# Batch 0 of a gated linear attention and mixer kernel: the transposed input of the MLP summed in PSUM, the low-rank part added in the second MLP bank, a matmul group split by parity, and a new order table

## The chip, the cores and the metric

The kernel runs on one core of a Trainium2 chip. Five engines work side by side, each through its own instruction list from front to end: TensorE (PE, with its weight loads PEld), VectorE (DVE), ScalarE (ACT), GpSimd (POOL) and SyncE (SP, which here only starts transfers). ACT also starts some transfers. The metric is the device time of one execution in microseconds, the median over runs.

## The reference, cut to what matters

```python
# per batch b (4) and head h (8), over t = 0..767, head width 48
state = alpha[t, :, None] * state + outer(k[t], v[t])
y[t]  = q[t] @ state
# x: (4, 768, 384), the eight heads' y side by side
h  = x.T @ U @ V            # over time, rank 32
u  = x + h.T
ch = relu(u @ w_ch1) @ w_ch2   # 384 -> 1536 -> 384
out = u + ch
```

## The kernel before, in words

Four batches go through the same stages. Batch 0 is done wholly, and batch 1 for its first four of six steps, in "pair units": one unit is 256 time steps of four heads, folded to 128 partitions. All else is done in plain chunks of 128 time steps and eight heads.

A unit (`stage_pair`, names in brackets are the kinds in the order table) takes four loads of 192 KB: alpha, k, q, v. ACT takes the logarithm of alpha [ln]; PE sums it over time in a PSUM bank [pcum]; ACT takes two exponentials and the decay factors [exp, ptot]; k and q are scaled [rk, rq] on POOL or DVE; PE transposes both [tr], ACT or DVE copies them out [kqev]; PE forms the scores in two banks, one for the even heads of the unit and one for the odd ones [psc]; DVE multiplies each bank by the mask into the two halves of `pm` [mask, twice]; PE multiplies `pm` by v and adds the part from the state [py, pyi]; the result is copied to `xb`, which holds x [pyev].

`stage_mix` then does the low-rank part of a batch: PE forms x^T U in a bank [xu], which is copied to `utx`; for each chunk of 128 rows PE multiplies by V into a bank [hb], and DVE adds x to it into `ub` [u]. PE transposes `ub`, six tiles to a bank [utr], ACT or DVE copies that to `uT` [uev]. Batches 2 and 3 transpose `ub` by transfers [tu]. `mlp1` takes w1 tiles times `uT`, three matmuls of 384 columns for each of 24 tiles of a batch, and ACT or DVE takes the relu of each into `h1`. `mlp2` sums twelve matmuls of 384 columns for a chunk, in three groups of four, and DVE adds `ub` and writes the output tile [out], which SP stores.

The w1 matrix comes in four loads of 576 KB, each for three of the twelve column tiles of w1. They land as f32 in the space of the other batch's `h1`; three casts each, on ACT or POOL, make bf16 of them. A tile of `mlp1` needs all three casts of its group. SP starts these loads amid those of q, k, v and alpha.

What stands where is set by hand-held data: `Plan.add` collects the operations with their dependences, and `run` emits them in the order of `TABLE`, three characters an operation, the last of which names the engine. `SLOTS` gives each buffer its place in its pool. An entry `++` emits filler matmuls (L270) into a bank that is free. No scheduler runs: each engine follows the table's order, and an operation whose input is late holds up all that stands behind it on its engine.

Lines of the profile: L270 filler, L389 to L396 [pcum], L428 [tr], L452 [psc], L486 [pd, the unit's state], L535 [py], L592 and L620 the same in plain chunks, L702 [xu], L716 [hb], L717 [u], L736 [utr], L765 [mlp1], L775 and L777 [relu], L791 [mlp2], L797 [out], L277, L279 and L281 copies on ACT, DVE and POOL, L320 the weight loads, L350 and L357 those of pair units and plain chunks.

Of the kernel before, what the change touches and what calls it, by code (L numbers as in the profile page):

```python
# [20 lines left out]
GFAAMSDMDALGDCPDDADmPDoPEQDESPD1AAQSDEABMSGJGDpAD3PGZAETDD5DDFPEUPDGDGIGDqAGbPDNPEVPGDGDOPD6P++BDsAGcADHDEWPEXAD4DD7PD8D
DPPDRAEYDGKPGMAD9PAYSGLPGNDACGADPD+PD-PEADGRPGSDDQAAEAEBAGOPGPDEZPEaPBTSGfGGwAGeAGdAEbAGyPG1ABNSGTD++BG0AEqPGQDBRSEoPGhP
GVPErDEkPGgGGWPGzABQAEcPEiPGjAEpDElDGiPGaGEsPHJAAUSAOGGXAEePEjDEtAAPGGkDGYAEdDHLPBOSHMAHNAEfDEmPGlPEnDANGGoPEgPGpDFGPGmD
GqDFHDFIPATABVSGnDFKPARGEhAFLAEwPExAASGFMPFNAE4PE2PAaGFQPE5DEyPBXSG2GBUSAZAFRDAbAFAPFJAE0PAcSE3ABSABZSFEPFFAGrDHOAG4PG6A
G3DHPDE1DFBAEuPHRPHTDFOPHQGEzDFPDG5PHiAFcPAXAFaPEvDG7AFdAAVAHSPHUDGsPGtPGuDBYSGvAG8PG+DAWGAhSBWSGxGGUGBaSAmSHVPBfSBrSG-P
FbAHkPHmAHoAFWPHADHBGE6PHXDH4AHnAFSPHlAG9DHqGFYPFTDH6PE7DH7AH8AHWDE+PHsPHuDHCDHpGE8PHKAFXAFZAHrPHtDFUPFVABbSE-AE9DHEPAgA
HFPHGPHYPHZDAfGBtSBjSHHDHvPHdPHIDHwDH+GIAPFCPAeGHaGAdAH9GHePFePHbDAiABcSHcDHxDICDFDAFkPF2PH-PIBDF8PIDPAlAHfPAjGAkGF9PBeS
HgAFwPBhSIFDHDGIEDHjABnSHyPH2PH3AH5AHzDH0DF3PFlPH1DIGPHhAApAFfPIHAIIPFxPIJAIQPISPAoGIKPAnGIRDITDAqGF+PFyPILDIMPINDFgPIYP
IZDF-DFzDF4PKCAKEPLBABkSIWPKFABzSJuAIXDIUPIOPIVAIPDKXAFmPFnDIaPBqSIbDJwPJxAF5DJ1DIiPKZPJvAIjAKdAI0PBlSFhDKGABdSAIGJyAJEP
JFABvSB1SIgPKKGJ2GI1AI+PI-AKIAIyPI4PKsAI5AIzAJGPIhDBiSI6PI7AJ0AJzAImPIqPKHAIrAInAKaAJKPIwPKDGJ+PJHAIkPKbAKuPKwAJIPLDPJLD  # L30
# [826 lines left out]
```

## Time and profile before

| what | value |
|---|---|
| runs | 159.13, 157.86, 158.62 us |
| median | 158.62 us |
| span of the profiled execution | 156.8 us |
| PE busy | 148.8 us (95%) |
| DVE, ACT, POOL busy | 107.6, 90.0, 61.4 us |
| moved by DMA | 31.53 MB |

The page gives the profiled execution by its span, from its first instruction to its last; a time of its own is not given. The median of the three runs lies 1.8 us above that span. A PE matmul is drawn with its pipeline, so that a row's mean duration is longer than what the next one has to wait; the spacing is read from the chain of waits, where a run of matmuls of one line stands as one piece.

### The profile page before, as it was taken

How to read it: one execution, taken by the hardware profiler on the slowest of the kernel's cores; microseconds unless marked ns; L12 is line 12 of the kernel's file. 1: busy time of each engine (PE TensorE's matmuls, PEld its weight loads, DVE VectorE, ACT ScalarE, POOL GpSimd, SP SyncE). 2: the span in 40 equal slices, each digit the busy share in tenths (PEclk: the TensorE clock that was granted, in tenths of full speed). 3: DMA queues.
4: the chain of work that ended last, by engine and by line, in shares of the span. 5: the costliest groups of instructions: out<-in, count | busy, mean ns of one | idle time of the engine just before them, and what ended most of it. 6: DMA issues, size and time to landing. Idle time of an engine off the chain costs nothing.

```text
span 156.8 us, 4413 instructions
## 1 busy us (share of the span) xinstructions
PE 148.8 (95%) x1715; PEld 97.7 (62%) x1715; DVE 107.6 (69%) x236; ACT 90.0 (57%) x234; POOL 61.4 (39%) x95
## 2 busy tenths in 40 slices
PE   2878999999999999999999999999999999999992
PEld 0456678666767656666668666665667555556662
DVE  6038899987899628816588976885989580673162
ACT  3678889986978272999958585379232202450000
POOL 8285995756088600136679261052623000000000
PEclk9999999999999999999999999999999999999999
DMA  5999999999988989989989996897976346345625
GB/s 145 319 323 326 268 301 313 344 265 268 280 239 193 270 161 191 189 169 211 208 169 214 134 222 119 169 181 145 176 144 151 105 87 139 127 129 151 199 100 201
DMA packets 98291, 31.53 MB, mean 201 GB/s; under 512 B 91968, under 2 KB 98240, under 8 KB 98272
## 3 DMA queue, kind: packets, MB, share of 16 engines
q1 hardware_dynamic: 92464, 29.11, 80.6%
q10 hardware_dynamic: 5808, 2.16, 5.2%
q8 instruction: 13, 0.21, 0.6%
q14 instruction: 6, 0.05, 0.1%
HBM read 23.79 MB, written 4.72 MB: 182 GB/s over the span
## 4 chain that ended last, share of the span: by engine, by line
PE 84%; DMA 8%; DVE 4%; ACT 1%; issue 1%; ACTq 0%; DVEq 0%
PE ps L791 30%; PE ps L765 29%; DMA io<-in_alpha_dram 8%; PE ps L716 3%; PE ps L620 3%; PE ps L592 2%; PE ps L687 2%; PE ps L428 2%; PE ps L535 2%; PE ps L558 2%; PE ps L682 1%; PE ps L736 1%; PE ps L452 1%; PE ps L643 1%; PE ps L702 1%; DVE rkq L411 1%
## 5 line engine op out<-in xcount | busy, mean ns | idle before, releaser
L791 PE MATMUL ps<-w_sb,h1t 128*128 128x384 bf16 (+2 forms) x300 | 53.1, 319 | 0.0
L765 PE MATMUL ps<-uT,w_sb 128*128 128x384 bf16 x288 | 51.0, 326 | 0.1
L775 ACT ACTIVATE h1t<-ps 128x384 bf16<-128x384 f32 x58 | 27.2, 509 | 19.1 <-PE ps L765 19.0
L791 PEld LDWEIGHTS <-h1t 128*128 128x128 bf16 x300 | 27.3, 97 | 15.9 <-issue 0.6
L765 PEld LDWEIGHTS <-w_sb 128*128 128x128 bf16 x288 | 27.0, 98 | 16.3 <-issue 0.4
L777 DVE TENSOR_SCALAR h1t<-ps 128x384 bf16<-128x384 f32 x38 | 20.1, 552 | 19.4 <-PE ps L765 15.9
L579 POOL TENSOR_TENSOR rkq<-io,aa 128x384 bf16<-128x384 f32 x12 | 11.7, 975 | 23.0 <-ACT aa L569 13.2
L630 DVE TENSOR_TENSOR pm<-ps,maskc 128x512 bf16<-128x512 f32 x28 | 17.7, 681 | 2.8 <-PE ps L620 2.8
L717 DVE TENSOR_TENSOR ub<-xb,ps 128x384 bf16<-128x384 bf16 x24 | 12.2, 549 | 6.9 <-PE ps L716 6.9
L797 DVE TENSOR_TENSOR io<-ub,ps 128x384 f32<-128x384 bf16 (+2 forms) x25 | 12.9, 531 | 3.7 <-PE ps L791 3.6
L277 ACT CAST xb<-ps 128x192 bf16<-128x192 f32 (+1 forms) x21 | 8.2, 393 | 10.6 <-PE ps L687 7.9
L463 DVE TENSOR_TENSOR pm<-ps,maskp 128x512 bf16<-128x512 f32 x20 | 13.2, 682 | 0.5 <-PE ps L452 0.2
L277 ACT COPY kqt<-ps 128x512 bf16<-128x512 bf16 x18 | 10.5, 608 | 1.6 <-PE ps L428 0.8
L579 POOL TENSOR_TENSOR rkq<-io,ai 128x384 bf16<-128x384 f32 x9 | 8.2, 914 | 6.9 <-PE ps L643 3.9
L411 POOL TENSOR_TENSOR rkq<-io,ai 128x384 bf16<-128x384 f32 x9 | 8.5, 945 | 6.1 <-ACT lt L380 3.1
L568 ACT ACTIVATE ai<-ps 128x384 bf16<-128x384 f32 x14 | 7.0, 502 | 5.6 <-PE ps L560 3.1
L654 POOL TENSOR_TENSOR st<-sm,tot 128x384 bf16<-128x384 f32 x8 | 6.9, 868 | 8.2 <-DVE sm L670 8.0
L571 ACT ACTIVATE tot<-ps,off 128x4 f32<-128x4 f32 x22 | 5.6, 279 | 5.3 <-PE ps L560 3.4
L279 DVE COPY kqt<-ps 128x512 bf16<-128x512 bf16 x18 | 7.3, 417 | 1.4 <-PE ps L592 0.9
L428 PE MATMUL ps<-ident,rkq 128*128 128x128 bf16 x80 | 8.0, 228 | 0.1
L281 POOL CAST w_sb<-h1t 128x384 bf16<-128x384 f32 x14 | 6.8, 516 | 2.9 <-DMA h1t<-in_moe_w_ch_dram 2.9
L411 POOL TENSOR_TENSOR rkq<-io,aa 128x384 bf16<-128x384 f32 x7 | 6.4, 910 | 3.4 <-ACT aa L404 2.3
(111 smaller groups left out, 224.5 us busy)
## 6 DMA issues: line engine op xcount, KB each, us to landing
io<-in_v_dram SPq DMA_DIRECT2D x22, 192.0 KB, 4.1
io<-in_q_dram SPq DMA_DIRECT2D x22, 192.0 KB, 4.4
io<-in_k_dram SPq DMA_DIRECT2D x21, 192.0 KB, 4.0
io<-in_alpha_dram SPq DMA_DIRECT2D x20, 192.0 KB, 4.3
out_dram<-io SPq DMA_DIRECT2D x13, 192.0 KB, 2.0
h1t<-in_moe_w_ch_dram SPq DMA_DIRECT2D x4, 576.0 KB, 6.0
h1t<-in_moe_w_ch_dram SPq DMA_DIRECT2D x3, 768.0 KB, 6.6
out_dram<-io SPq DMA_DIRECT2D x20, 96.0 KB, 2.2
```

The source lines that it names most:

```text
L277: nc.scalar.copy(dst, src)
L411: eng.tensor_tensor(jh(dst()[:, :, 0:D]), raw(a), jh(x()), op=ALU.mult)
L428: nc.tensor.matmul(dst, lhsT=ring()[:, HP * j + 2 * a : HP * j + 2 * a + 2, :].rearrange("t h w -> t (h w)"), rhs=ident, start=True, stop= ...
L463: nc.vector.tensor_tensor(dst, s2, maskp.to_broadcast([C, 2, 2, C]), op=ALU.mult)
L579: eng.tensor_tensor(dst()[:, :, 0:D], a(), x(), op=ALU.mult)
L630: nc.vector.tensor_tensor(pm()[:, :, par, :], s2, maskc.to_broadcast([C, HP, C]), op=ALU.mult)
L717: P.add(f"u {b}.{c}", lambda e, c=c, hb=hb: nc.vector.tensor_tensor(ub()[:, c, :], xb()[:, c, :], hb()[:, 0:DM], op=ALU.add), r=[hb] + xk( ...
L765: nc.tensor.matmul(hb()[:, 0:TW], lhsT=w1_sb[:, ct, jt * 128 : (jt + 1) * 128], rhs=u_half(uT, ct, tt, b in QUEUE_U), start=(ct == 0), sto ...
L775: nc.scalar.activation(dst, hb()[:, 0:TW], AF.Relu)
L777: nc.vector.tensor_scalar_max(dst, hb()[:, 0:TW], 0.0)
L791: nc.tensor.matmul(hb()[:, 0 : hi - lo], lhsT=h1()[:, jt, c * C : (c + 1) * C], rhs=w2_sb[:, jt, lo:hi], start=(jt == 0), stop=(jt == NJ - 1),
L797: P.add(f"out_{hi - lo} {b}.{c}", lambda e, hb=hb, lo=lo, hi=hi: nc.vector.tensor_tensor(flat(ou)[:, lo:hi], ub()[:, c, lo:hi], hb()[:, 0 ...
```

## The change

For batch 0 alone (`INPLACE = (0,)`), `u` is no longer formed. For each half of the time steps (`tt`) and each third of the width (`j`) a bank takes three matmuls of x against the identity, which transpose it [xt, L723], then one matmul of 384 columns with `utx` as weights and V as moving data, which adds the low-rank part already transposed [ht, L728]; the bank is copied to `uT` [xtev]. The six [hb], six [u], three [utr] and three [uev] of that batch fall away. The low-rank part that `out` needs is put into the bank of `mlp2` ahead of its twelve matmuls, by one more matmul of 384 columns a chunk [hbo], and `out` adds x in place of u. `utx` gets a third buffer.

In all pair units [py] is split in two operations, one for the even and one for the odd heads, so that each needs one half of `pm`. Number and shape of its matmuls stay.

`TABLE` and `SLOTS` are new throughout: engines of copies, scalings, casts and loads are chosen anew too. There are three fillers where there were eleven, 43 operations on POOL's rk and rq where there were 37, and 22 loads are started by ACT where there were 11.

```diff
 TABLE = """
-ArA++BAASAvSA-AA3SQPAAySAsSCLA++BCNPAtSAzA++BA5ACOACPAAwS++BCiADSAECAAxSBAACRGAuS++BCSGCjACQACkPA4SClA++BCmAA7ADUPDVADWA
+AASAFGArAQfACLA++CCNPAsSCOACRDAGPAJPAvSAHDCjAClPCTPCPACQACnAAtSA3SDVAAuSCMGCaPCSDCUPCmAAxSCqGAzSC7AAySCVDAKDCkAAwSCpGA4S
...
+    INPLACE = (0,)
...
-    utxs = Pool(slots("utx", 2, [128, DM], BF16))
+    utxs = Pool(slots("utx", 3, [128, DM], BF16))
...
-        def f_y(e):
-            for h in range(HP):
+        def f_y(e, par):
+            for h in range(par, HP, 2):
...
-        P.add(f"py {b}.{u}", f_y, r=[rv, (pm, 0), (pm, 1)], w=[yb[0], yb[1]])
+        for par in range(2):
+            P.add(f"py {b}.{u}", lambda e, par=par: f_y(e, par), r=[rv, (pm, par)], w=[yb[0], yb[1]])
...
+        if b in INPLACE:
+            for tt in range(2):
+                for j in range(NCT):
+                    tb = Buf(bank)
+
+                    def f_xt(e, tt=tt, j=j, tb=tb):
+                        for n in range(NT):
+                            nc.tensor.matmul(tb()[:, n * C : (n + 1) * C], lhsT=xb()[:, tt * NT + n, j * C : (j + 1) * C], rhs=ident, start=(n == 0), stop=False, skip_group_check=True)
+
+                    P.add(f"xt {b}.{tt}.{j}", f_xt, r=[x for n in range(NT) for x in xk(b, xb, tt * NT + n)], w=[tb])
+                    P.add(
+                        f"ht {b}.{tt}.{j}",
+                        lambda e, tt=tt, j=j, tb=tb: nc.tensor.matmul(tb()[:, 0:TW], lhsT=utx()[:, j * C : (j + 1) * C], rhs=ve_sb[:, tt * TW : (tt + 1) * TW], start=False, stop=True, skip_group_check=True),
+                        r=[utx, ("ve", tt)], w=[tb],
+                    )
+                    P.add(f"xtev {b}.{tt}.{j}", lambda e, tt=tt, j=j, tb=tb: copy(e, uT()[:, j, tt * TW : (tt + 1) * TW], tb()[:, 0:TW]), r=[tb], w=[(uT, "t", tt, j)])
+            return utx
...
+            if b in INPLACE:
+                P.add(f"hbo {b}.{c}", lambda e, hb=hb, lo=lo, hi=hi: nc.tensor.matmul(hb()[:, 0 : hi - lo], lhsT=(ve_sb if paired(b, c) else vm_sb)[:, c * C : (c + 1) * C], rhs=utx()[:, lo:hi], start=True, stop=False), r=[utx, ("ve" if paired(b, c) else "vm", c // NT)], w=[hb])
...
-                            start=(jt == 0), stop=(jt == NJ - 1),
+                            start=(jt == 0 and b not in INPLACE), stop=(jt == NJ - 1),
...
-            P.add(f"out_{hi - lo} {b}.{c}", lambda e, hb=hb, lo=lo, hi=hi: nc.vector.tensor_tensor(flat(ou)[:, lo:hi], ub()[:, c, lo:hi], hb()[:, 0 : hi - lo], op=ALU.add), r=[hb, (ub, c)], w=[(ou, n)])
+            P.add(f"out_{hi - lo} {b}.{c}", lambda e, hb=hb, lo=lo, hi=hi: nc.vector.tensor_tensor(flat(ou)[:, lo:hi], (xb if b in INPLACE else ub)()[:, c, lo:hi], hb()[:, 0 : hi - lo], op=ALU.add), r=[hb] + (xk(b, xb, c) if b in INPLACE else [(ub, c)]), w=[(ou, n)])
```

Three places show what the new order does. DVE, in the stretch that leads to batch 0's `mlp1`: before (`pm` masks of a unit of batch 1, `ub` the sums of x and the low-rank part, `uT` a copied transpose).

```order
L463 TENSOR_TENSOR pm_193<-ps,maskp 128x4x128
L717 TENSOR_TENSOR ub_205<-xb_202,ps 128x384 x4
L279 COPY kqt_192<-ps 128x512
L717 TENSOR_TENSOR ub_205<-xb_202,ps 128x384 x2
L279 COPY uT_210<-ps 128x2x3x128
```

The same place now, where `uT` is copied straight from the bank in which it was summed:

```order
L464 TENSOR_TENSOR pm_193<-ps,maskp 128x4x128
L280 COPY kqt_191<-ps 128x512
L464 TENSOR_TENSOR pm_193<-ps,maskp 128x4x128
L280 CAST uT_211<-ps 128x384 x2
L502 TENSOR_TENSOR st_198<-ps,tot_186 128x192
```

The six sums are gone from DVE, and two of the six narrower copies stand there; the other four are ACT's.

SP's loads around the four of w1 (`h1t` is where they land; the `io` tiles are inputs of batch 1). Before, the row with x2 holds column groups 0 and 1, the next weight row group 3, the last one group 2:

```order
L350 DMA io_166<-in_v_dram 128x4x96
L350 DMA io_167<-in_alpha_dram 128x4x96
L320 DMA h1t_73<-in_moe_w_ch_dram 128x3x384 x2
L350 DMA io_168<-in_k_dram 128x4x96
L320 DMA h1t_73<-in_moe_w_ch_dram 128x3x384
L357 DMA io_169<-in_alpha_dram 128x8x48
L350 DMA io_170<-in_q_dram 128x4x96
L350 DMA io_171<-in_q_dram 128x4x96
L320 DMA h1t_73<-in_moe_w_ch_dram 128x3x384
```

Now, with the groups in the order 3, 2, 1, 0:

```order
L351 DMA io_168<-in_v_dram 128x4x96
L321 DMA h1t_73<-in_moe_w_ch_dram 128x3x384
L351 DMA io_169<-in_q_dram 128x4x96
L321 DMA h1t_73<-in_moe_w_ch_dram 128x3x384
L358 DMA io_170<-in_alpha_dram 128x8x48
L351 DMA io_171<-in_k_dram 128x4x96
L321 DMA h1t_73<-in_moe_w_ch_dram 128x3x384
L351 DMA io_172<-in_v_dram 128x4x96
L321 DMA h1t_73<-in_moe_w_ch_dram 128x3x384
```

The last w1 load was SP's 34th transfer after that of V, and is now the 42nd. Ahead of it stood 29 input loads of 192 KB on SP and ten on ACT; now 37 stand ahead of it on SP and two on ACT, and three more of ACT stand around the first tiles of batch 0's `mlp1`.

POOL's casts of w1 (`w_sb`), among scalings of batch 1 (`rkq`). Before:

```order
L281 CAST w_sb<-h1t_73 128x384 x6
L411 TENSOR_TENSOR rkq_81<-io_168,ai_184 128x8x48
L411 TENSOR_TENSOR rkq_79<-io_171,aa_179 128x8x48
L281 CAST w_sb<-h1t_73 128x384
L281 CAST rv_178<-io_173 128x384
```

Now:

```order
L282 CAST w_sb<-h1t_73 128x384 x2
L412 TENSOR_TENSOR rkq_80<-io_169,aa_180 128x8x48
L282 CAST w_sb<-h1t_73 128x384 x5
L282 CAST rv_178<-io_172 128x384
L412 TENSOR_TENSOR rkq_78<-io_171,ai_183 128x8x48
L282 CAST w_sb<-h1t_73 128x384 x2
```

Nine of the twelve casts of w1 stand on POOL now, in three pieces; the last piece of two is of group 0, whose load comes last. In PE's list the first tile of group 0 is the fourteenth of batch 0's 24 tiles of `mlp1`; before, it was the first.

More of the change, by code (lines that the diff above doesn't have):

```diff
@@ L21 @@
[L21 to L30, printed above, removed]
@@ new lines @@
+DfDCvPChAC-ABASDKPCzD++BC0PDePDxPDzAEJPDBGBBSDLPCwDDgDDhPCxDC1DDpPDyADMDDNPDjDEKAD0AGOADDPEMADFABCSDODDCGDEPDGDDkPELADWG
+DlPDmDDiDGQPGSADHPGmADqPD2GD4PD6ADIDDrPDsPGTADJDDnPDoDENGEPPERDGoPEOGEQPC2PDuAABSESDEWPDtAEIGA8SEXPGqAD1GBESEYDGRAC3PC4P
+GpAETPGrAEZPACGC5ADQPC6DD3PEUDEaPD+PDPPDRPD5AA+SDwGBPSHYAEVDDSPDTADUAEbPBFSBGSD-PEADGUGD7PD8DEcPEdAEeAADPAEABLSBISD9DEBP
+GWPGYDHaPECPGVGGXPEDPG+AGPGGdPHcAEEPEGDGZDHAPALGEFAEfPEgPHbAGeDGfDGaPGbDGsGHDAEuPEhAGuPGwDBOSG-GGhPGcDBMSHBABKSHCAHEGHdA
+EiPEjPEvPEkAEwAEoPEpPEqDExPEyPEzAAYSErPEsPEtDGnGAZABJSElPEmPG1PG2DAUSGiPGjPBTSBQSHNPGgDHODG3DG4DHPDHQDAQSHGPAaGAbGFgPBSS
@@ new lines @@
+AMSBXAGkAFePEnAGtGAWGAVGHIAGlAFKPFfAGvPFIPGxDFiPFJDFjDBNSFGPBVAGyPAXGFhDBRAHyAH0PH2AH1AGzDFaPFAPBYSFcPBZSG0DFYPFLAFHDFdD
+FBAASAFbAFCPFDAARGATGE8PBUSE9DHZGHeGAPAIIAFZDAOGE6PG5PG6PANGG7PG8DH3AHFGHnPE7DFQPHRGHfGHoDFRDIKPAcSFSPBfABWAG9AHpDIMAH6D
+FTAFOPFPAHgPHiDHHPILAHqDH4AE+PHhPHJDFMPHjAH8PH+AE-DAhSFNAE2PE3AAmSHkPHKPHMDHTPBaSE4PE5AH5GE0PE1AINGHlDAfAHmDIOGFUPFVAIPP
+FWPHLDFXAIRDAeGAgGH7PH9DBkSHsPAdGFEPIQPISDFFAHtPHSPHzGKSAHuPHvPHrGHxDH-PIADHUPHVPAkGBlAHWAITPIVDBjAHXDHwAIBDBrSGAPGBPAlA
+BbSBiSBcSBmSGHPGIPKUPKYAAjAICPIEDAiGBgSFyPFzPAoAFkPIGPIHAKXAIDDGCPFlPAnGFmPIUDIFGIJAKVAIWPIXDAqGApGFnPGDPGEDIYPFrPFsPFoD
@@ new lines @@
+LRAKnABhABzSKpPIZDBdSF5PKqAKsAFtPJ+AKrAKvGKtAIgPIhDIiPFuPGJPKAPKDAIjDGKPKxPAIGIoPKZGKuGFvDLTPBvSKBAIpDKzDGLDBwABeSKWALUA
+B7ALWABsSF6PKCAIkPIlDKbPKdDF0PImPKEAF7PKFGKHPKwPInDKGGKJDLmAF8PF9DJ-AKTGBtSBuSBnSIqPIrDIaPIbDLoPLqALpABqSKiPKyDNVAF1PKOP
+LVALXAKaGJQPKIPKKAKPDGNSIcPJGPJRDIdDKjDF2DLYGLrGK9GLSGJHABoSJEPJFAJIPKLPJJALZGB1SKNDK0PKMDKcPKeDK1DB6AFxSBxSLsGB+AIePB4S
+KoAIfAB-SB3SJUPJaPJWPJbAKkDLaPLcAK8AJOPIwPK2DJXDJKPJLDIxAKfPJPAKhDK+PLCAKQPKRDKgDK-AN4AIuPNXPNaAIvAJYPJZDNZALAAIyPIzDI4P
+K3PK6PK4DLBABpSI+PKlPLDGLMPK7AB9SCDSI5DI-ANnGLFPLHDI0PJVAK5GNbALNDB8SLbPLdDKmDIsPLtPLvDLuPLEGLOGNdGI1DItDB0ANYANcGByALnG
@@ new lines @@
+LwDCEAB2ACGAJMPLhPI6POKACASI7AJSPGGSLiDJTALGPN6PN8AOAGLIDI2PI3DCBSCCSJuPB5SNeSF-SCHSJNAN7AN+ALePLfDLJPLxPLzDLLDLKDJvPLyD
+N-DJ0PJCPJDAJAPJwPCIAJBAOMPOQALjGLPPLgDOPAJ1PN9ALkPL0POcAONAOdAJxDJzSL1AJ2PJcPORGLlDLQDOOAL2PNmAOBSJ3DJ4SI8PNoPNWGFwSCFS
+L3DMEPMCPNqAJ5PMFDNsAMDDMGSI9DL-PNpAMADL9PL6PJ6PJdPNrAL+DN5ANtDMBSL4PL5DL7DL8SFqSOuAJePJfDOCPNfPNgDJ7PCJANiPOEDJiPJ8DJjP
+OSGOLGNjDCKAOwPOxANzPNhDN0DOyAOePNuGNvSN1DODDJkPJoPJpPJqPJrDMNPJlDOTSJySJnSMPPGMSMjPMkDOFPMQAOIPOGDOiAOhAOvGO0GOgAOkGOJA
+OXPOzGMODMvPMdPOHDMeAMtPMuAMlPMmAOYDJgSOfAOjGMJPOZGMwAMxPMyDNwPMKAOUPNkPMZPOVDMVPMbPMzPMcAOWDNyDNxDMfPMRPJ9SMSAM1PNlDM0D
@@ new lines @@
+OaPObDMaDMgAJhSMTPOpPMXPO1SO2PMWAOqDOrGOlSM2AOmPOoDGFSMYAMhPO4DO3DMLPMrPMiANQPMpPN2PO5PMMDOnDN3DMnPO6DOsPNLPMqANGPMsAOtA
+MoANHPO7PO8DMHPMUAMIDNMPF+SPCPPHPPEPPIDPJPPKDPLSNIPPDDPFDNJDPGSO9PM3PM4PO-PPADNRPM5PNNPO+DPBSM8PNSPM9PM+PM-DNASNTDPmPPaP
+JtSM6DPMPPNAP4PP5APnAPuPPvAPbAPSPFpSPePNBPPqPPkPPoPPlAPpDPrAPiPPYPPZAPjDPgPPcPPdAPhAPOPPsPJsSPfDPPDPQPPyPPWPNCPNDPPUPPtD
+P2PJmSPTAPRDQBPPzAPXDNUSNEDNFSF4SPVDP6PF3SQGPP7APwPP3ANKSPxDQaPP8PP9PP0PP1AQbPP+PP-DQASQVPQWPQXPNODNPSQYDQHPQIPQJDQKSQZS
+QcPM7SQdDQCPQDPQEDQFSQeSQLPQMPQNPQODQPSQQPQRPQSPQTDQUS
@@ L52 @@
+DDGCAHBBeCEfghEDGCCiAABAEDBGHAAjDCBAkBFEDmBGHAClnABBDCECFDCECCABGFEAHADCABBABGBAEDFBBFGEAHDHCFBBDAGDGCAFABIBNDLMKHADCSEB
+CBCCGJPFWDYCCDABECHGCADGCOEACGHCAAEUADABBBZFHBVCCGBEBDCDBBCAAGCdHFDBAbGBCRDBiACDACFCDEgGfABAADHBBABACBECBAADAAHCGBEADFCC
+GHABDEHBFAEBDBBDDGHACCAEHCBDAGBCEADGAFCEAhDAEGcnFCkEADGHAEDFGCFDGCFAGDCFHlAGDECAFFmCINDDGA
 """
@@ L756, in mlp1 @@
             hb = Buf(bank)
-            if b in QUEUE_U:
+            if b in INPLACE:
+                need = [(uT, "t", tt, j) for j in range(NCT)]
+            elif b in QUEUE_U:
                 need = [(uT, "c", c) for c in ((0, 1), (1, 2))[tt]]
@@ L779, in mlp1, with mlp2 @@
             P.add(f"relu {b}.{tt}.{jt}", g, r=[hb], w=[(h1, tt, jt)], after=casts[jt] if b == 1 else ())
-    def mlp2(b, ub, h1, c):
+    def mlp2(b, ub, h1, c, xb, utx):
         tt = c // NT
@@ L819 @@
                 whole = [(x, 0, x)]
-        stage_mix(b, xb, ub, uT)
+        utx = stage_mix(b, xb, ub, uT)
         mlp1(b, uT, h1, 0)
@@ L823 @@
         for c in range(NC):
-            mlp2(b, ub, h1, c)
+            mlp2(b, ub, h1, c, xb, utx)
     P.add("table", lambda e: nc.scalar.preload_act_table_set("natural_log_exp_and_others"))
```

29 lines of the change are left out of this document (6 added, 23 removed).

## The prediction

> **What bounds the kernel now.** I read the stretches first, then PE's groups, then the chain of waits, and last the engines' own lines around the start of batch 0's `mlp1`. The stretches (us; busy us and instructions of each engine; clock; DMA share; GB/s):
>
> ```profile
> 0.00:4.00 4.00, 1.04 (x2) 0.24 (x3) 2.44 (x21) 1.56 (x2) 3.26 (x16) 1.00 0.54 148
> 4.00:8.00 4.00, 3.64 (x21) 1.83 (x21) 0.12 (x2) 2.35 (x6) 0.92 (x3) 1.00 1.16 320
> 8.00:12.00 4.00, 3.20 (x41) 2.49 (x40) 1.24 (x2) 3.14 (x10) 3.22 (x5) 1.00 1.17 324
> 12.00:16.00 4.00, 3.51 (x84) 2.53 (x81) 3.29 (x8) 3.49 (x10) 2.40 (x3) 1.00 1.17 324
> 28.00:32.70 4.70, 4.70 (x92) 3.53 (x90) 4.69 (x12) 4.38 (x13) 3.69 (x8) 1.00 1.15 327
> 32.70:40.00 7.30, 7.25 (x52) 4.43 (x50) 5.77 (x12) 5.37 (x13) 4.13 (x6) 1.00 1.07 248
> 40.00:49.30 9.30, 9.30 (x158) 6.63 (x156) 8.66 (x21) 8.24 (x23) 4.83 (x8) 1.00 0.93 247
> 49.30:154.00 104.70, 104.68 (x1001) 67.43 (x997) 69.60 (x135) 50.87 (x133) 29.67 (x39) 1.00 0.79 167
> 154.00:156.80 2.80, 0.00 (x0) 0.00 (x0) 0.30 (x1) 0.00 (x0) 0.00 (x0) 0.98 0.40 140
> ```
>
> From 32.70 on PE is never free, and until then the DMA engines are full at about 325 GB/s: one load of 192 KB is 0.61 us of them, one w1 load of 576 KB 1.8 us. So there are two parts. From the first `mlp1` matmul to 154 each us of PE work is a us of span. Ahead of it the time is that of loads and of the chain behind them, and PE work is covered.
>
> ```profile
> L765 PE MATMUL ps<-uT,w_sb 128*128 128x384 bf16 x288 | 51.0, 326 | 0.1
> L270 PE MATMUL ps<-h1t 128*128 128x512 bf16 x10 | 4.6, 519 | 1.4 <-DVE h1t L201 1.2 <-ACT ve_sb L277 0.2
> ...
> L463 DVE TENSOR_TENSOR pm<-ps,maskp 128x512 bf16<-128x512 f32 x20 | 13.2, 682 | 0.5 <-PE ps L452 0.2
> ...
> 31.44 0.36 PE ps L736 x6
> 31.80 0.35 PE ps L452 x16
> 32.15 0.28 PE ps L486 x8
> 36.94 0.33 issue
> 37.27 0.35 DVE st L501
> 40.34 0.22 PE ps L428 x4
> 41.85 0.30 PE ps L535 x16
> 43.00 0.27 PE ps L558
> 58.22 0.49 PE ps L716 x3
> 64.70 5.87 PE ps L765 x36
> ```
>
> The rows from 31.44 on are pieces of the chain (start, us, what). They give the spacing: a matmul of 384 columns is 0.163 us (L765, 36 in 5.87; L716, three in 0.49), a transpose of 128 about 0.06 (L736, six in 0.36). In the saturated part the chain leaves PE only from 36.94, for about half a us as PE's own count shows: 32.70 to 40.00 holds 13 `mlp1` tiles of 0.49 and two transposes of four, 6.8 of 7.3 us.
>
> What leads to 32.70 is the low-rank part of batch 0 (start, us, engine, line):
>
> ```profile
> 27.29 0.50 PE L702 MATMUL ps<-xb,ue_sb 128*32 128x384 bf16 x6
> 28.02 0.53 ACT L277 CAST utx<-ps 128x384 bf16<-128x384 f32 x1
> 28.96 1.95 DVE L717 TENSOR_TENSOR ub<-xb,ps 128x384 bf16<-128x384 bf16 x4
> 31.16 1.00 DVE L717 TENSOR_TENSOR ub<-xb,ps 128x384 bf16<-128x384 bf16 x2
> 32.08 0.55 DVE L279 COPY uT<-ps 128x768 bf16<-128x768 bf16 x1
> 32.35 0.51 PE L736 MATMUL ps<-ident,ub 128*128 128x128 bf16 x6
> 29.61 2.31 POOL L281 CAST w_sb<-h1t 128x384 bf16<-128x384 f32 x5
> 32.62 0.51 POOL L281 CAST w_sb<-h1t 128x384 bf16<-128x384 f32 x1 [0.71 <-DMA h1t<-in_moe_w_ch_dram]
> 36.62 0.50 POOL L281 CAST w_sb<-h1t 128x384 bf16<-128x384 f32 x1 [0.69 <-DMA h1t<-in_moe_w_ch_dram]
> ```
>
> From x^T U (27.29) to the first tile (32.70) are 5.4 us, and the six sums of DVE fill the middle. The casts of group 0 are among the five done by 31.9, so weights did not hold the first tile. The last two rows date two landings: the third w1 load at 32.6, the fourth at 36.6; the chain shows nothing that waited for its group.
>
> **The change part by part.**
>
> *Transpose in PSUM.* Eighteen transposes and six matmuls of 384 columns go, eighteen transposing matmuls of 128 columns and six of 384 come: even, 0 us of PE. Whether a matmul against the identity without the transpose form keeps 0.06 us no row shows; a matmul's spacing goes with its columns in the rows above, and both ends (0 and double, +1.0 us) lie ahead of the first tile, where PE has cover. DVE loses 2.95 us of sums. Copies: three of 768 columns go, six of 384 in f32 come; their nearest row is `utx`'s 0.53, four on ACT, two on DVE. The chain gets x^T U 0.5, `utx` 0.53 after its gap of 0.2, six sums in PSUM with the transposes between them, about 2.0 (six of 0.163 and eighteen of 0.06), and a last copy 0.53: 3.8 us for 5.4. If x^T U starts no earlier, the chain allows a first tile at 31.1; with some of the tightening of [py], 30 to 31.
>
> *[hbo].* Six matmuls of 0.163 in the saturated part: +0.98 us, with no cover. DVE's `out` reads x for u: 0.
>
> *[py] by parity.* The same matmuls. The first half may start one mask (0.68 us, the L463 form) earlier in each unit, at most that, and only ahead of 32.70 does it count; it lies in the 30 to 31.
>
> *Fillers.* Eight fewer of at most 0.52 us each (L270), all ahead of the first tile, in PE's waits: 0 in the sum, if the clock stays (below).
>
> *PE work moved over the first tile.* The scores of one unit of batch 1 (L452 x16, 0.35) go behind it, the state of another (L486 x8, 0.28) ahead: +0.07.
>
> *Order of the w1 loads.* This is the term that decides; two more views are needed, the transfers' medians from issue to landing and ACT's copies.
>
> ```profile
> io<-in_alpha_dram ACTq DMA_DIRECT2D x4, 192.0 KB, 4.4
> io<-in_q_dram ACTq DMA_DIRECT2D x2, 192.0 KB, 5.0
> h1t<-in_moe_w_ch_dram SPq DMA_DIRECT2D x3, 768.0 KB, 6.6
> ...
> L277 ACT COPY kqt<-ps 128x512 bf16<-128x512 bf16 x18 | 10.5, 608 | 1.6 <-PE ps L428 0.8
> ```
>
> Ahead of the last w1 load stood 39 loads and three w1 loads, and it landed at 36.6. Now 37 of SP and five of ACT are ahead, for ACT's last three stand at the first tiles, near 30, and take 4.4 to 5.0 us to land. Three loads more are 0.59 MB: 1.8 us at 327 GB/s, 2.4 at the 248 of that stretch. So it lands at 38.4 to 39.0; if ACT's three fall behind it, 36.6. I take 38.7, since the DMA engines have no free time there. Two casts on POOL, 0.5 each, follow: group 0 is ready at 39.7. POOL is free for them: ahead of them stand a cast (0.5) and a scaling whose last load is the one before, 1.8 us earlier.
>
> The first tile of group 0 is PE's fourteenth. Ahead of it, from the first tile, lie 13 tiles of 0.49 (6.36), one transpose group (0.22), one group of scores (0.35), a prefix sum (0.27), the last product (0.30), a state (0.28) and a state part of about 0.1: 7.9 us. The first tile itself needs group 3, which is behind 35 loads, as the third w1 load was before, but behind two w1 loads fewer, 1.18 MB or 3.6 us at 327: landed at 29.0, cast by 30. So PE starts at 30 to 31, is at the fourteenth tile at 38 to 39, and waits for 39.7. The wait is 1 to 2 us, and any start before 31.8 (39.7 less 7.9) ends the same.
>
> *The sum, against the profiled execution.* Start as if at 31.8 in place of 32.70: -0.9. Before's own half us at 36.94 falls in the same place and is covered by the wait: -0.5. [hbo] +0.98, moved work +0.07. Together -0.35: span 156.4. The tail from 154.0 keeps its 2.8 us (one sum and one store). The page gives no time of the execution besides the span; the median of the runs is 1.8 above it, which I add: 158.3 us.
>
> Queues passed: the first w2 load waits for the same casts, since it lands in the space that w1 leaves; at the 6.6 us above it is there at 46.3 and cast by 48. Between the fourteenth tile and w2's first use lie eleven tiles (5.4 us) and, by the chain's rows, some 4 us of batch 1: 49. It holds nothing up. What is queued on ACT behind its cast of group 0: a logarithm, two exponentials and relus; see below.
>
> **The rivals.**
>
> *The weights come in time* (faster). If the loads ahead land at 36.6, as the 39 before did, group 0 is ready at 37.6, which is before PE gets there from 30. Then -2.7 for the start at 30, -0.5 (the scalings on DVE behind 36.94 stand on POOL now), +1.05: span 154.6, 156.4 us; from a start at 31, 157.4. For it: three loads of another queue need not be served in order of issue. Against it: DMA shares above 1.0 throughout.
>
> *ACT held by a cast* (slower). ACT's cast of group 0 stands ahead of a logarithm, exponentials and relus of tiles of batch 0. ACT then waits from about 36 to 38.7, and in 40.00 to 49.30 it was busy 8.24 of 9.30, so 1.1 us can be made good there. If it makes that good, 1.6 us remain in which tiles lie in banks unread and PE stops, 159.9; if nothing, 2.7, 161.0. I take the middle, 160.5. It decides, past 160.2, if ACT makes good less than 0.8. Against it: half of [kqev], 0.61 each, went from ACT to DVE.
>
> *PE stays slow at the start* (slower). The prefix sum's first matmul, 384 columns, at four times:
>
> ```profile
> 7.73 0.53 PE L389 MATMUL ps<-lt,upto 128*128 128x384 bf16 x1
> 9.59 0.48 PE L389 MATMUL ps<-lt,upto 128*128 128x384 bf16 x1
> 11.44 0.32 PE L389 MATMUL ps<-lt,upto 128*128 128x384 bf16 x1 [0.21 <-ACT lt L380]
> 14.03 0.32 PE L389 MATMUL ps<-lt,upto 128*128 128x384 bf16 x1
> ```
>
> Until 9.6 us it takes 0.16 us more, which is its 384 columns at half speed, though the clock column shows 1.00; six fillers stand ahead of the row at 7.73 on PE. Now two do. If half speed lasts to 16, the work of 12 to 16, at most the 3.51 us that PE was busy, is doubled: x^T U at most 3.5 late, the first tile at 33.5 to 34.5, no wait for weights left, so +0.8 to +1.8 with -0.5 and +1.05: span 158.2 to 159.2, time 160.0 to 161.0. Half speed to 14 costs half of that and vanishes in the wait; it decides from about 16. For it: fewer fillers. Against it: real matmuls keep PE occupied from 8 on.
>
> [...]
>
> **How the numbers follow.** The forecast, the weights eating the gain: 0.52, 158.3 us, its own range 157.0 to 159.9. Weights in time: 0.26, 156.4. ACT held: 0.12, 160.5. Slow PE: 0.10, 160.5. A measurement here can tell a change of about 1% from none, which is 157.0 and 160.2. Faster by over 1%: 0.20 from the second case and 0.07 from the first. Slower: 0.15 from the last two, 0.05 from the first. Within 1%: 0.53. The range 156.0 to 160.8 leaves out the far ends of the second and of the last two, together 2 in 10.
>
> **What would show it.** Right: DVE's L717 at 18, PE's L765 line starting at 30 to 31, a wait of PE of 1 to 2 us about 8 us after it, ended by POOL's or ACT's cast of w1 and behind that by a w1 load landing near 38.7, and PE unbroken from there. Wrong: no such wait (weights in time), a first tile after 32, L389 still at 0.48 past 12 us, relus of ACT late after a cast, or PE waits after 55, for which no term stands here.

## The result, and the profile after

The changed kernel takes 169.88 us (median of four runs, 169.36 to 170.23), the kernel before 158.38 beside it: a ratio of 1.070, 95% interval 1.064 to 1.076. It is slower by 11.5 us. The span went from 156.8 to 167.9 us. Ratios with an interval are of fast runs alone, medians of all runs.

The stretches of the changed kernel, in the columns of the table before, cut at the new start of `mlp1` and behind it:

```profile
31.36:40.00 8.64, 7.96 (x70) 4.47 (x72) 6.89 (x15) 5.20 (x13) 4.97 (x10) 1.00 1.13 313
40.00:49.30 9.30, 7.57 (x109) 4.87 (x109) 6.45 (x16) 6.26 (x16) 6.99 (x10) 1.00 0.99 267
49.30:70.00 20.70, 20.49 (x238) 13.65 (x236) 13.62 (x30) 11.45 (x32) 11.58 (x19) 1.00 1.10 225
70.00:85.00 15.00, 14.51 (x172) 9.96 (x172) 12.68 (x26) 11.06 (x30) 8.24 (x11) 1.00 1.02 206
85.00:100.00 15.00, 10.06 (x95) 6.22 (x92) 7.41 (x15) 4.62 (x14) 4.42 (x6) 0.77 1.02 183
100.00:167.90 67.90, 65.00 (x548) 40.47 (x544) 39.29 (x75) 20.81 (x51) 9.51 (x12) 1.00 0.49 110
```

Before, PE was busy 104.68 of 104.70 us from 49.3 to 154. Now one stretch stands out: from 85 to 100 PE is idle for 4.94 us, executes 95 matmuls where the stretch ahead of it, as long, has 172, and its granted clock is 0.77. The page says the same in its summary of the chain that ended last and in its row of clocks, 4.2 us a digit:

```profile
PE 47%; DMA 24%; SPq 20%; ACT 3%; issue 2%; POOL 1%; DVE 1%; ACTq 1%; DVEq 0%
...
PEclk9999999999999999999997599999999999999999
```

PE carried 84% of that chain before and DMA 8%; now PE has 47%, and transfers with the queue that starts them 44%.

PE's own rows around the hole (start, us, and in brackets the idle time ahead):

```profile
86.85 0.81 PE L814 MATMUL ps<-w_sb,h1t 128*128 128x384 bf16 x4
92.50 1.75 PE L622 MATMUL ps<-kqt 48*128 48x128 bf16 x24 [4.84 <-ACT h1t L796]
94.18 2.74 PE L814 MATMUL ps<-w_sb,h1t 128*128 128x384 bf16 x8
96.71 1.24 PE L786 MATMUL ps<-uT,w_sb 128*128 128x384 bf16 x6
97.79 0.81 PE L814 MATMUL ps<-w_sb,h1t 128*128 128x384 bf16 x4
```

Two losses stand here. PE waits 4.84 us for a PSUM bank that an ACT relu (L796) must read first. Behind the wait eight `mlp2` matmuls take 2.74 us, and four take 0.81 when they run at full speed: 0.32 us from one to the next where 0.16 is usual. About 1.9 us are lost to half speed until 96.8.

Why is the relu late? ACT's rows; ACTq is ACT starting a transfer:

```profile
82.59 0.43 ACTq L358 DMA_DIRECT2D io<-in_k_dram  x1
83.07 0.49 ACT L570 ACTIVATE ai<-ps 128x384 bf16<-128x384 f32 x1 [0.24 <-issue]
84.86 0.42 ACTq L358 DMA_DIRECT2D io<-in_v_dram  x1
87.56 0.44 ACTq L358 DMA_DIRECT2D io<-in_k_dram  x1
89.32 2.18 ACTq L358 DMA_DIRECT2D io<-in_v_dram  x2
91.55 0.52 ACT L553 ACTIVATE lt<-io 128x384 bf16<-128x384 f32 x1 [7.99 <-DMA io<-in_k_dram]
91.97 0.85 ACT L796 ACTIVATE h1t<-ps 128x384 bf16<-128x384 f32 x2
```

ACT computes nothing for 7.99 us. It has five loads of 192 KB to start for batches 2 and 3, and from the second on each start waits. The chain of waits shows for what (start, us, what):

```profile
82.69 4.85 DMA io<-in_k_dram
87.54 0.02 issue
87.56 3.99 DMA io<-in_k_dram
91.56 0.03 ACT lt L553
```

A load that SP started at 82.69 lands at 87.54, and 0.02 us later ACT starts its third. The other three fit as well: transfers of SP land at 84.84, 89.30 and 91.10, and ACT starts at 84.86, 89.32 and 91.12. In the built program each load carries a wait on one of eight completion counters, which the transfers of SP and ACT share:

```
157 L358 DMA io8_142<-in_k_dram 128x8x48 [waits DMAHW0_49]
159 L358 DMA io13_147<-in_v_dram 128x8x48 [waits DMAHW2_49]
160 L358 DMA io11_145<-in_k_dram 128x8x48 [waits DMAHW4_49]
161 L358 DMA io12_146<-in_v_dram 128x8x48 [waits DMAHW6_49]
162 L358 DMA io10_144<-in_v_dram 128x8x48 [waits DMAHW1_49]
163 L553 ACTIVATE lt2_77<-io2_136 128x8x48 [waits Activation_49]
```

So each of these starts waited until an earlier holder of its counter had landed. The two loads in the chain took 4.85 and 3.99 us to land, at a DMA share of 1.02 in the stretches from 70 to 100 us. Behind the five starts stand on ACT a logarithm, three relus and two exponentials, and behind those PE.

The ledger uses PE's delay: the start of an operation less all PE work ahead of it in the order, each operation priced at the usual spacing of its matmuls. Where PE never waits it stays flat. Before, it is 13.5 at the first `mlp1` tile, 13.7 at 45 us, 14.0 at 78 and 14.2 at the end. After, it is 12.3 at the first tile, 15.7 at 45, 16.9 at 83, 21.9 behind the long wait, 23.8 behind the half speed and 24.2 at the end. These 10.0 us more and the 0.98 of added work ([hbo]) give 11.0 of the 11.1 us by which the span grew.

### The profile page after: what moved, and what is told of

It reads as the page before. It is cut to its first block, busy times and chain, and to the rows that moved or that the text cites. A ratio compares the mean times of both kernels' runs of the same rounds, so it can differ in the third digit from the quotient of the medians.

```text
span 167.9 us, 4420 instructions
## 1 busy us (share of the span) xinstructions
PE 151.4 (90%) x1714; PEld 98.7 (59%) x1714; DVE 109.6 (65%) x242; ACT 82.1 (49%) x214; POOL 67.6 (40%) x106
## 4 chain that ended last, share of the span: by engine, by line
PE 47%; DMA 24%; SPq 20%; ACT 3%; issue 2%; POOL 1%; DVE 1%; ACTq 1%; DVEq 0%
PE ps L814 21%; PE ps L786 17%; SPq L358 11%; DMA io<-in_q_dram 8%; SPq L351 7%; DMA io<-in_v_dram 6%; DMA io<-in_k_dram 5%; DMA h1t<-in_moe_w_ch_dram 3%; DMA out_dram<-io 2%; PE ps L622 2%; PE ps L689 1%; ACT h1t L796 1%; SPq L321 1%; PE ps L735 1%; PE ps L684 1%
## 5 line engine op out<-in xcount | busy, mean ns | idle before, releaser
L786 PE MATMUL ps<-uT,w_sb 128*128 128x384 bf16 x288 | 54.0, 327 | 1.7 <-POOL w_sb L282 1.1
L796 ACT ACTIVATE h1t<-ps 128x384 bf16<-128x384 f32 x60 | 27.0, 495 | 33.8 <-PE ps L786 33.7
L814 PEld LDWEIGHTS <-h1t 128*128 128x128 bf16 x300 | 28.3, 99 | 16.9 <-issue 1.2
L581 POOL TENSOR_TENSOR rkq<-io,aa 128x384 bf16<-128x384 f32 x13 | 12.5, 963 | 14.0 <-ACT aa L571 10.0
L820 DVE TENSOR_TENSOR io<-ub,ps 128x384 f32<-128x384 bf16 (+2 forms) x19 | 9.7, 530 | 12.5 <-PE ps L814 12.4
L282 POOL CAST rv<-io 128x384 bf16<-128x384 f32 x18 | 9.0, 504 | 16.8 <-PE ps L689 10.1
L581 POOL TENSOR_TENSOR rkq<-io,ai 128x384 bf16<-128x384 f32 x12 | 10.7, 913 | 9.9 <-ACT ai L570 5.8
L553 ACT ACTIVATE lt<-io 128x384 bf16<-128x384 f32 x14 | 7.3, 528 | 13.0 <-DMA io<-in_k_dram 10.0
L280 DVE COPY kqt<-ps 128x512 bf16<-128x512 bf16 x27 | 11.2, 418 | 3.2 <-PE ps L594 1.4
L736 DVE TENSOR_TENSOR ub<-xb,ps 128x384 bf16<-128x384 bf16 x18 | 9.2, 549 | 3.6 <-PE ps L735 3.4
L622 PE MATMUL ps<-kqt 48*128 48x128 bf16 x112 | 5.3, 235 | 4.9 <-ACT h1t L796 4.8
L412 POOL TENSOR_TENSOR rkq<-io,ai 128x384 bf16<-128x384 f32 x9 | 8.2, 913 | 3.6 <-ACT xb L278 2.1
L280 DVE CAST xb<-ps 128x384 bf16<-128x384 f32 (+1 forms) x14 | 6.6, 481 | 4.7 <-PE ps L689 4.1
L412 POOL TENSOR_TENSOR rkq<-io,aa 128x384 bf16<-128x384 f32 x9 | 8.7, 970 | 1.1 <-DMA io<-in_q_dram 1.0
```

The source lines that it names most:

```text
L280: nc.vector.tensor_copy(dst, src)
L282: nc.gpsimd.tensor_copy(dst, src)
L412: eng.tensor_tensor(jh(dst()[:, :, 0:D]), raw(a), jh(x()), op=ALU.mult)
L581: eng.tensor_tensor(dst()[:, :, 0:D], a(), x(), op=ALU.mult)
L786: nc.tensor.matmul(hb()[:, 0:TW], lhsT=w1_sb[:, ct, jt * 128 : (jt + 1) * 128], rhs=u_half(uT, ct, tt, b in QUEUE_U), start=(ct == 0), sto ...
L796: nc.scalar.activation(dst, hb()[:, 0:TW], AF.Relu)
```

## The experiments

Entries of the order table have three characters; the last names the engine (A for ACT, S for SP, P for PE). Ratios are to the kernel before.

**Is ACT held by the loads that it starts?** Three kernels hand such loads to SP. First all of ACT's loads but its first:

```diff
-A1A BXA BVA BRA BfA BWA BlA BjA BhA BwA B7A B6A B+A B0A ByA CEA B2A CGA CIA CJA CKA
+A1S BXS BVS BRS BfS BWS BlS BjS BhS BwS B7S B6S B+S B0S ByS CES B2S CGS CIS CJS CKS
```

> The changed kernel, with all loads but the first one started by SP (22 by ACT before, 1 now); order and all else as they were. Theory one: the lost time comes from ACT standing still on transfers that it is to start (8.0 us idle before a logarithm at 91.5 us), which holds relus, so banks, so PE (4.8 us) and then PE's speed. Then the 4.8 us wait of PE and the half-speed stretch behind it go, and the time is 159 to 162 us. Theory two: the loads of batches 2 and 3 are late whoever starts them, since the DMA engines are full until about 100 us. Then the wait stays under another name and the time is 167 to 171 us.

Measured: 168.25 us, 1.060 (1.055 to 1.065), in the range of theory two. The wait for ACT is gone, and PE has a new one at another product:

```profile
PE ps L622 <- DMA kqt<-rkq: 2.0, 1, 2.0
```

That is a transposing transfer of batch 3, started by SP behind the loads that it took over. A wait was traded.

The last eight only (those that start from 82 us on):

```diff
-B0A ByA CEA B2A CGA CIA CJA CKA
+B0S ByS CES B2S CGS CIS CJS CKS
```

> The changed kernel, with only the last eight of ACT's loads (from 82 us on) started by SP. Theory one: the wait of 4.8 us, the half speed behind it (about 2 us) go and the early losses stay: 161 to 164 us. Theory two: no change, 168 to 171 us.

Measured: 166.15 us, 1.046 (1.041 to 1.051), between the ranges of the two theories. In the profiled execution, which took 170.27 us, the 4.84 us are gone, and PE waits 4.3 us in three pieces for the same transposing transfers.

The six early ones only:

```diff
-A1A BXA BVA BRA BfA BWA
+A1S BXS BVS BRS BfS BWS
```

> The changed kernel, with only ACT's loads 2 to 7 (between 9 and 42 us) started by SP. If ACT's and SP's waits for one another's transfers are what makes the last w1 load late (40.9 us), the fourteenth tile of batch 0 starts up to 2 us earlier than its 42.0, and the time falls to 167 to 169 us at most, for the later wait stays. If the w1 loads are late for want of bandwidth alone, the tile stays at 41 to 42 and the time at 169 to 171 us.

Measured: 165.47 us, 1.042 (1.037 to 1.047), less than either forecast. The last w1 load lands at 39.1 us in place of 40.9, and the fourteenth tile starts at 40.16 in place of 41.98, as the first reading said. PE's delay is 14.6 at 48 us, where it was 15.7, but the larger gain comes late: the wait at the same product is 2.06 us in place of 4.84, and no half speed follows.

All three gain, none gets near the kernel before.

**The new parts or the new order?** The table was rebuilt twice: the old order with the new operations in the places of those that they replace, and the new order with the old way of building u.

```diff
-    INPLACE = (0,)
+    INPLACE = ()
```

(The line is of the second kernel, which has [hb], [u], [utr] and [uev] of batch 0 where [ht] and [xtev] stood. In the first, `INPLACE` stays and all of `TABLE` is that of the kernel before, save for these operations.)

> The changed kernel's parts (u transposed in PSUM for batch 0, its low-rank part added ahead of batch 0's second MLP, the pair units' last product in two) in the order of the kernel before: each new operation stands where the one stood that it takes the place of, and everything else, the loads above all, where it stood. Order theory (the 11 us come from the new order, whose products of batches 2 and 3 stand earlier than their loads can arrive): near the kernel before, the six added low-rank products (+0.98 us) less what the transposes save, 157.5 to 159.5 us, no wait of TensorE over 2 us after 60 us. Rival (the new parts themselves cost it, by banks held or evictions that come late): most of the loss stays, 164 to 170 us.

> The new order without the new way of building u: batch 0's u is made as before (low-rank product, add on VectorE, transpose, copy) at the places of the new operations, and no low-rank products stand ahead of the second MLP; the split product stays. Order theory: 166.5 to 170 us, with TensorE's wait of 3 to 5 us near 88 to 92 us. Rival (the new parts cost it): 157 to 161 us.

Measured: the old order with the new parts 160.96 us, 1.016 (1.012 to 1.020); the new order without them 168.53 us, 1.053 (1.045 to 1.060). The first is a little slower than was expected. PE's delay in it is 1.0 higher at the end than before, nearly all of it there by 33 us, and the six [hbo] matmuls are the other 0.98 of the 2.0 us of span. PE never waits over 1 us behind 31 us. The second has PE's wait (3.2 us) at the same product and starts that product at 92.30, where the changed kernel starts it at 92.50, though PE came there 1.4 us later. The release comes near 92 us in both, whenever PE gets there.

**Which loads, and is it their amount?** Three of the five loads were moved on ACT behind the logarithm, relus and exponentials:

```diff
-CEA B2A CGA (behind LwD)
+CEA B2A CGA (behind N+A)
```

> The changed kernel with three of the five loads that ScalarE starts one behind the other at 82.6 to 91.5 us (k and v of batch 3's piece 4, v of its piece 0) moved on ScalarE behind the logarithm, the relus and the exponentials that stood behind them. Held-engine theory (ScalarE is held by loads that it must start and that wait for an earlier transfer's completion): TensorE's 4.84 us wait and the half speed behind it go or shrink to under 1.5 us, and the time falls by 4 to 6.7 us to 163.2 to 166. Supply theory (the transfers themselves arrive too late for this order, whoever starts them): the wait reappears at another product of batch 2 or 3 by 3 us or more, and the time stays above 167.

Measured: 165.3 us, 1.041 (1.035 to 1.047), within the first theory's range. The product starts at 87.10, with no wait, and the eight matmuls behind it take 1.47 us. But 3 us later:

```profile
87.10 0.84 PE L622 MATMUL ps<-kqt 48*128 48x128 bf16 x24
87.88 1.47 PE L814 MATMUL ps<-w_sb,h1t 128*128 128x384 bf16 x8
...
93.77 0.33 PE L684 MATMUL ps<-st,kqt 128*128 128x96 bf16 x4 [2.56 <-ACT h1t L796]
...
96.25 2.33 PE L814 MATMUL ps<-w_sb,h1t 128*128 128x384 bf16 x8
```

The moved loads now hold the next relus, as ACT's rows show:

```profile
90.83 0.37 ACTq L358 DMA_DIRECT2D io<-in_k_dram  x1
91.25 1.89 ACTq L358 DMA_DIRECT2D io<-in_v_dram  x2
93.23 0.49 ACT L796 ACTIVATE h1t<-ps 128x384 bf16<-128x384 f32 x1 [5.69 <-DVE io L820]
```

They were moved on, behind those too:

```diff
-CEA B2A CGA (behind LwD) ... CIA (behind JwP) ... OdA
+JBA CEA B2A CGA CIA (behind JwP) ... OdA (behind NmA)
```

> As the run with three of ScalarE's loads moved behind its relus, but they and a fourth (k of piece 5) moved further, behind the two relus (columns 10 and 11 of batch 1's first half) that came late in that run, and the copy of piece 4's v behind the next logarithm. Held-engine theory: the wait of 2.56 us at 91.2 us and the half speed behind it go too, the time falls by another 2.5 to 4 us to 161.3 to 162.8. Supply theory: the loads that start later are now waited for themselves, by sums of batch 3, the time stays within 1 us of 165.3.

Measured: 166.26 us (163.06 to 166.83; too spread for a ratio), against the expectation of 161.3 to 162.8; it is within 1 us of 165.3, as the supply theory said. That wait went as well, and PE then waited 2.15 and 0.68 us at x^T U of batch 2, with half speed behind it. With the six early loads on SP besides:

```diff
-A1A BXA BVA BRA BfA BWA
+A1S BXS BVS BRS BfS BWS
```

> That kernel with ScalarE's six loads of 9 to 42 us started by SyncE as well, as in the run that moved these alone. If the early loads hold ScalarE as the late ones do, some 0.6 to 1.1 us more are gained (TensorE's delay at 48 us was 14.6 us there against 15.7): 160.3 to 162. If SyncE's queue only passes the wait on: the same as the kernel with ScalarE's loads left there, within 0.6 us, or longer.

Measured: 169.36 us, 1.074 (1.066 to 1.082): 3 us above the median of the run before it, whose spread is wide. PE waits 1.2 us at 48.0, 1.2 at 58.2 and 1.1 at 71.3, and it is busy for 13.91 of the 15 us from 70 to 85, all of which it filled in the run before. That SP's queue passes the waits on fits this; no single transfer is shown to do it.

Four output stores that the new order puts among the loads were left out:

```diff
-GNS ... FxS ... GGS ... F-S
```

> The changed kernel without the four output stores that SyncE starts at 71.5 to 91.7 us among the loads (half the rows of four pieces of batch 0 are not written). Supply theory (the new order's stores among the loads take transfer time that the loads of batches 2 and 3 need): three stores of about 0.6 to 0.7 us each stand ahead of the load whose landing lets ScalarE go at 91.1 us, the wait falls from 4.84 to about 2.9 us, and the time falls by 2 to 3 us (167 to 168). Rival (order of issue, not the amount): the time stays within 1 us of 169.9.

Measured: 170.09 us, 1.070 (1.064 to 1.077), no gain, as the rival said; the product starts at the very same time, 92.52, behind a wait of 5.79 us. These stores are 96 KB each, 0.4 MB in all. As a test of the amount it was too small: the run with half loads below takes away 3.5 MB.

**Where in the order?** The two orders were crossed at entry 428, at about 51 us: new then old, and old then new. In a third only the start is new, up to the first `mlp1` products.

```diff
-HxD H-P IAD HUP HVP AkG BlA HWA
+HxD H-P IAD HUP HVP AkG BrS BbS BtS BjS HWD HXD FkP FlP
```

(The rows around the crossing of the first; the others are cut the same way.)

> The changed kernel in its new order up to its first MLP products only (about 31 us), everything behind in the order of the kernel before. If the loss lies in the later part, as the waits at 88 us suggest: near the run with the old order throughout (160.96 us), 158.5 to 162, less if the MLP's earlier start is kept, more if the first weights then come late as in the changed kernel (40.9 us). If the start is guilty: 165 us or more.

> The new order for its first 428 entries (to about 51 us), the old one behind. Later-part theory: 160 to 163.5 us, with the 1.5 to 2 us that the changed kernel lost by 47 us (late weights) and no wait of TensorE over 2 us after 55 us. Early-part theory: 166 us or more.

> The crossing the other way: the old order for its first 428 entries (to about 51 us), the new one behind. Later-part theory: 165 to 169 us, with waits of 3 us or more in all of TensorE between 80 and 105 us. Early-part theory: 159 to 162 us.

Measured: new then old 161.19 us, 1.015 (1.008 to 1.021); old then new 169.90 us, 1.070 (1.061 to 1.078), 0.9 us above the forecast range, with a wait at the same product, which starts 0.6 us earlier than in the changed kernel:

```profile
91.88 1.75 PE L622 MATMUL ps<-kqt 48*128 48x128 bf16 x24 [3.92 <-ACT h1t L796]
```

So the loss lies behind 51 us. The kernel with only the start new missed its expectation: 170.13 us, 1.063 (1.055 to 1.071). The crossing at 31 us parts the first weight loads from what waits for them, and PE stood still there:

```profile
40.12 8.83 PE L786 MATMUL ps<-uT,w_sb 128*128 128x384 bf16 x36 [5.06 <-POOL w_sb L282]
```

That loss is of the crossing's own making. It still says two things: 36 of these matmuls took 8.83 us in place of 5.87, so behind the wait of 5.06 us half speed cost 2.96 us more; and behind 50 us, in the old order, PE's delay grew by only 0.4.

**Is it the transfers?** The loads of q, k and v for batches 2 and 3 were cut to half the heads, in the changed kernel and in the one before.

```diff
-dma_start(t(), src[b, :, sl, :].rearrange("h t d -> t h d"))
+dma_start(t()[:, 0:HP, :], src[b, 0:HP, sl, :].rearrange("h t d -> t h d")) if b >= 2 and src is not alpha else ...
```

> The changed kernel with the loads of q, k and v for batches 2 and 3 cut to half the heads (36 of their 48 loads move half their bytes; the other half of each tile keeps what stood there). Transfer theory: no wait of TensorE over 1 us behind 60 us and no half speed, TensorE's delay stays at the 16 to 17 us it had at 70 us: 160 to 162.5 us. Rival (the order waits on banks, evictions or chains of small steps whatever the transfers do): 166 us or more.

> The same cut in the kernel before, whose TensorE runs through from 40 us on: within 0.7 us of the kernel before (157.7 to 159), since nothing there waits for these loads.

Measured: 161.11 us for the changed kernel, 1.015 (1.006 to 1.024), and 159.08 for the one before, 1.003 (0.998 to 1.008), which is 0.1 us past its forecast. The stretches of the first:

```profile
49.00:70.00 21.00, 21.00 (x247) 14.16 (x245) 13.91 (x31) 12.37 (x35) 12.52 (x21) 1.00 0.97 200
70.00:85.00 15.00, 15.00 (x182) 10.39 (x180) 13.89 (x30) 11.71 (x30) 9.24 (x13) 1.00 0.73 145
85.00:100.00 15.00, 15.00 (x167) 9.31 (x165) 12.81 (x25) 7.37 (x21) 5.46 (x8) 1.00 0.79 133
```

PE is busy through all three, at clock 1.00, in the changed order, with ACT's loads where the change put them. ACT's five loads, in its rows:

```profile
80.41 0.37 ACTq L358 DMA_DIRECT2D io<-in_k_dram  x1
80.86 0.49 ACTq L358 DMA_DIRECT2D io<-in_v_dram  x1
81.39 0.52 ACTq L358 DMA_DIRECT2D io<-in_k_dram  x1
81.94 1.08 ACTq L358 DMA_DIRECT2D io<-in_v_dram  x2
83.07 0.52 ACT L553 ACTIVATE lt<-io 128x384 bf16<-128x384 f32 x1 [1.26 <-issue]
```

They are started in 2.6 us; it was 8.9. The transfers of batches 2 and 3 are worth 8.8 us to the changed order and nothing to the old one.

**Is the half speed a thing of the wait?** Fillers were put ahead of the waiting product to keep PE at work.

```diff
-N+A LeP
+N+A ++U LeP
```

> The changed kernel with 20 filler matmuls of 512 columns (as at the start, results not read) ahead of the product that waited 4.84 us from 87.66 us, so that TensorE works through the wait. Clock theory (TensorE runs at half speed for some 4 us behind the idle wait, since it was idle): fillers end about when the wait ended, the eight L814 matmuls behind them take about 1.35 us and not 2.74, the time falls by 1.5 to 2.2 us to 167.7 to 168.4. Rival (the half speed has another cause, such as the traffic at that time): the L814 matmuls keep 2.7 us, the time stays within 0.5 us of 169.9 or is longer.

> As the run with 20 fillers, but these read the weights of the first MLP, which nothing writes any more, so that they need not wait for the relu. Clock theory: they run from 87.7 us on at about 215 ns each, end at about 92.0, the eight L814 matmuls behind the wait take about 1.35 us and not 2.74, and the time falls by 1.5 to 2.2 us to 167.7 to 168.4. Rival (the half speed comes from the traffic of that time): the L814 matmuls keep 2.7 us and the time stays at 169.4 or above.

> The 20 fillers once more, on the first MLP's weights and into the one PSUM bank whose last reader (an add on VectorE) was done before the wait, so that nothing of ScalarE stands ahead of them. Clock theory: they start at about 87.7 us, run at about 215 ns each and end at about 92.0; the products behind them (24 of L622, eight of L814) take 0.8 to 0.9 and about 1.4 us and not 1.75 and 2.74; the time falls by 1.5 to 2.2 us to 167.7 to 168.4. Rival (half speed from the traffic of that time, whatever TensorE does): those products keep 1.75 and 2.74 us and the time stays at 169.4 or above.

The first two missed: 173.78 us, 1.096 (1.089 to 1.103), and 173.63, 1.088 (1.079 to 1.097). The fillers waited themselves, for a tile or a bank that the late relus held, and ran behind the wait:

```profile
92.80 0.59 PE L271 MATMUL ps<-h1t 128*128 128x512 bf16 x1 [4.84 <-ACT h1t L796]
93.61 5.93 PE L271 MATMUL ps<-h1t 128*128 128x512 bf16 x18 [0.22 <-issue]
```

They took the half speed on themselves, 427 ns each until 97.4, then 216. In the third kernel they ran in time:

```profile
87.56 4.48 PE L274 MATMUL ps<-w_sb 128*128 128x512 bf16 x20
93.88 0.78 PE L625 MATMUL ps<-kqt 48*128 48x128 bf16 x16 [1.84 <-ACT h1t L799]
...
95.36 1.47 PE L817 MATMUL ps<-w_sb,h1t 128*128 128x384 bf16 x8
```

The release came at 93.88 there, later than in the changed kernel, and the eight matmuls behind it took 1.47 us and not 2.74. Here the PE that was kept busy kept its speed. The time did not fall by what was expected: 169.96 us at the median, but its four runs lie between 166.72 and 171.14, too far apart for a ratio. The kept speed is shown in the trace, its worth in the time is not.

No kernel tried beats the one before.

## Why the prediction was wrong

The prediction was 158.3 us, "same" at 0.53, range to 160.8. The time is 169.88, outside the range and slower than each rival.

**The step that failed** is the frame of the sum: that from the first `mlp1` matmul "each us of PE work is a us of span". It was read from 104.68 busy us in 104.70, which hold for the old order. They were carried over to an order that is new throughout, and nothing in the sum asked whether the loads of batches 2 and 3 still come in time. The text had the test for it ("or PE waits after 55, for which no term stands here") and no price. What the runs showed in its place: the order behind 51 us costs 8.7 us (161.19 against 169.88), and as much goes when the loads of batches 2 and 3 are halved in the same order (161.11), so the loss is that of late transfers.

How much the order asked for could have been counted. By the priced PE work ahead of them, the last `mlp2` product of batch 0 moved from 69 to 53 us of work, the first transposes of batch 2 from 58 to 48, its first scores from 64.4 to 56.6. The work that needs no load was spent early, and the work that needs loads was asked for 8 to 10 us sooner. The DMA engines had nothing to spare: their share is 1.02 to 1.10 in the stretches from 49 to 100 us. In the trace batch 2's last load lands at 89 us, where it was 83, and by 89 us 13 loads of batch 3 and two stores have landed, against 10 and none.

**The loads of ACT** were counted (22 for 11) but priced only where they pass the w1 loads. That a start can hold all of ACT behind it was in none of the terms. The rival of ACT held looked at a cast near 38 us.

**Start of `mlp1`**: 30 to 31 forecast, 31.36 measured. The size was nearly right, the reason is not borne out: with the new parts in the old order it stands at 33.68, and with the new order but the old parts at 34.13, both later than the 32.70 before. Only both together pulled it forward: it stands at 30.85 to 32.57 in eleven kernels with this start, and at 33.97 and 34.63 in two more (new then old, and the last eight loads on SP). The spread is wide: the kernel before with half loads, whose start is untouched, has it at 34.14.

**Weights**: a wait of 1 to 2 us at the fourteenth tile, behind POOL's cast, was forecast. PE waited 1.07 us there:

```profile
41.98 0.66 PE L786 MATMUL ps<-uT,w_sb 128*128 128x384 bf16 x3 [1.07 <-POOL w_sb L282]
```

The mechanism was right, and that the size lies in the range is luck: the load landed at 40.9 and not at 38.7, and PE, with small waits of its own, came to the tile at 40.9 and not at 38 to 39. SP started that load at 33.05, and three loads that ACT started from 30.80 to 33.39 were under way beside it (they landed at 37.67, 41.09 and 41.64). With ACT's early loads on SP those three start behind it; it starts at 33.26 and lands at 39.09, which is still later than the 36.6 that the prediction gave for that case. SP was also held from 34.55 to 37.75, by a counter that an ACT load gave back at 37.67, but that came behind the start of the last w1 load and can only have delayed later loads. With smaller waits nearby, PE's delay at 45 us is 2.0 above that before, where the start and the wait together were priced at -1.4.

**[hbo]**, +0.98: the old order with the new parts has six matmuls of 0.163 more and shows just that beside its 1.0 at the start.

**PE slow at the start**: the first matmul of the prefix sum takes 0.53 us at 10.85 and 0.32 at 14.95 (the next one follows after 0.32 and 0.17), so the half speed lasted somewhat longer than before and cost nothing that can be seen. Later it was not cheap at all: 1.9 us behind the long wait. The wait at the fourteenth tile did not slow PE: three matmuls in 0.66 us behind the 1.07. Short waits do not rule half speed out, though: in the profiled execution of new then old the longest wait of PE is 1.9 us, the granted clock is 0.89 over the first 31 us, which makes some 6.8 us at half speed (twice 0.11 of 31), and the first `mlp1` tile started at 33.97. That is a loss of the kind that this rival named.
